# A decode block's last weight row: 640 columns by nine GpSimd transfers to twenty partitions

## The chip, the core and the metric

The kernel runs on one core of a Trainium2 chip. The metric is the time of one execution on the device in microseconds (us). The profile's span runs from the first to the last instruction of one profiled execution.

## What is computed

One decode step of a transformer block: layernorm, grouped attention over a long cache, output projection and residual, then layernorm, a gated feed-forward part and residual. Cut to what matters here:

```python
def _B_ref(x, w_gate, w_up, w_down):
    return (_gelu(x @ w_gate) * (x @ w_up)) @ w_down

h  = x + _A_ref(_layernorm(x), k_cache, v_cache, wq, wo)   # one token, 32 heads over 65536 keys of 4 kv heads
h2 = h + _B_ref(_layernorm(h), w_gate, w_up, w_down)       # D = 1024, F = 3584, all bf16
```

Nearly all of the work is to read the cache and the weights once: 173 MB. `w_down` has 3584 rows of 1024 columns.

## The kernel before

SyncE issues nearly all loads, in the order of use: `wq`, then key and value chunks of 4 to 8 MB, `wo`, `w_gate`, `w_up` and `w_down`. They go through a ring of four 32 KB slots in each partition. Each load is issued as soon as the reader of its slot is done, so several stand in the queue ahead of their use. The attention is a loop of eight steps on TensorE, VectorE and ScalarE. An explicit list of operations with semaphores (`Flow`) sets the order up to the gate matmuls; from line 583 on the order of each engine is the order in the text.

The end of the program is what the change touches:

- `w_down` is laid out as 28 rows for each of 128 partitions. `FA` = 16 of them form `wa`, the other `FB` = 12 `wb_src`, of which the first `FM` go to `wb` and the last `FZ` - 1 to `w_end`. The twelfth, `last_row`, is split by columns at `EC` = 640.
- Columns 640 to 1023 of `last_row` come first in SyncE's queue, by four transfers of three partitions with ten slots each and two of four partitions (line 600, semaphore 0). They lie in `w_odd`, on partitions 0 to 11 in eleven slots, in the memory of the transposed keys (`over` places a tensor there). Row 12 s + m of the 128 is slot s of partition m.
- Then come `wa` (semaphore 1, 4096 KB), `wb` (semaphore 2), two rows of `w_end` (semaphore 3), and columns 0 to 639 of `last_row` on 128 partitions (semaphore 4, 160 KB).
- When `up` has landed, 64 matmuls (L646) make its product, VectorE turns it into columns (L623) and multiplies it into `actz` (L649), the activations.
- For `w_odd` the activations of the last row have to be moved: `s_of` and `g_of`, made at the start from the identity, tell for each partition its slot and its place. VectorE masks (L682), one matmul gathers (L683), VectorE copies into `a_odd` (L684), and eleven matmuls (L689) use it.
- `down_wide` (L669): 32 matmuls, 512 wide, on `wa`, into the bank `e_ps`. ScalarE copies the bank into `e_sb` (L694), while `stay_busy` runs three matmuls whose result nobody reads (L662). `add_wide` (L675) folds `e_sb` into the output banks with four fp32 matmuls, which the trace shows as eight.
- `down` (L657): 128-wide matmuls into the output banks, eight for each row of 1024 columns, so 72 for nine rows, 16 for two and 5 for the last 640 columns. Each group waits for its own semaphore.
- Two copies (L704, L705) and a store (L706) end the program.
- GpSimd at that place clears `actz` (L618) and makes `to_row` and `h_of` (L615 to L617), on which the matmul of L637 waits. That matmul stands ahead of the 64 of L646 on TensorE.

Of the kernel before, what the change touches and what calls it, by code (L numbers as in the profile page):

```python
# [9 lines left out]
ALU = mybir.AluOpType  # L10
AX = mybir.AxisListType
BF16 = mybir.dt.bfloat16
# [106 lines left out]
def kernel(  # L119
# [13 lines left out]
    nc = tc.nc  # L133
    P = 128
# [7 lines left out]
    FC = F // P  # L142
# [13 lines left out]
    NB = 512  # L156
# [8 lines left out]

    FZ = 3
    w_end = nc.alloc_sbuf_tensor("w_end", [P, FZ, D], BF16)
# [14 lines left out]
    def sb(name, shape, dtype=F32):  # L182
        return const.tile(shape, dtype, name=name)
# [3 lines left out]
    qs = sb("qs", [P, 4, NS, P + 1], BF16)  # L187
    sc = sb("sc", [P, CPH, NN, rep, NS])
    pt = sb("pt", [P, CPH, NN, rep, NS], BF16)
    bank = [psum.tile([P, NB], F32, name="bank%d" % i) for i in range(8)]  # L190
    kt_bytes = ktb[:].rearrange("p c s w -> p (c s w)")

    def over(offset, shape, dtype=F32):

        n = 1
        for x in shape:
            n *= x
        if dtype == F32:
            v = kt_bytes[:, offset // 4:offset // 4 + n]
        else:  # L200
            v = kt_bytes[:, offset // 4:offset // 4 + n // 2].bitcast(BF16)
        if len(shape) == 2:
            v = v.rearrange("p (a b) -> p a b", a=shape[0])
        return v
# [5 lines left out]
    op = f.op  # L210
# [4 lines left out]
    k_sem = [tc.alloc_semaphore("k_landed_%d" % i) for i in range(DCH)]  # L215
    end_sem = [tc.alloc_semaphore("end_landed_%d" % i) for i in range(5)]

# [38 lines left out]
    GN = 3 * GP  # L256
    GS = P // GN
    left = GS * GN
    ident_w = sb("ident_f", [P, GN * (GS + 1)])
    ident_f = ident_w[:, 0:P]  # L260

    def select(key, out, op_, fill, base, pattern, mult, rows=None):
# [14 lines left out]
       in_=ident_f.rearrange("p (q m) -> p q m", q=4).unsqueeze(2).to_broadcast([P, 4, NI, SQ]))  # L277
# [8 lines left out]
    op("dve", "tensor_reduce", r=["ident_f"], w=["mine"], out=mine[:], in_=ident_f.rearrange("p (i c) -> p i c", i=NI), axis=AX.X, op=ALU.add)  # L286
    g_of = sb("g_of", [P, GN], BF16)
    s_of = sb("s_of", [P, GS + 1], BF16)
    op("dve", "tensor_reduce", r=["ident_f"], w=["g_of"], out=g_of[:], in_=ident_w[:].rearrange("p (s m) -> p m s", m=GN), axis=AX.X, op=ALU.max)
    op("dve", "tensor_reduce", r=["ident_f"], w=["s_of"], out=s_of[:], in_=ident_w[:].rearrange("p (s m) -> p s m", m=GN), axis=AX.X, op=ALU.max)  # L290
    sel16 = sb("sel16", [P, 16])
# [288 lines left out]
    with tc.tile_critical(no_gpsimd_drain=True):  # L580
# [15 lines left out]
    loads += [(wa, B_w_down[0:P * FA, :].rearrange("(p e) n -> p e n", p=P), 1), (wb[:, 0:FM, :], wb_src[:, 0:FM, :], 2),  # L596
              (w_end[:, 0:FZ - 1, :], wb_src[:, FM:FB - 1, :], 3), (w_end[:, FZ - 1, 0:EC], last_row[:, 0:EC], 4)]
    landed = [0] * 5
    for dst, src, i in loads:
# [17 lines left out]
    nc.gpsimd.tensor_tensor(out=h_of, in0=h_col[:].unsqueeze(1).to_broadcast([P, 16, DC]), in1=sel16[:].unsqueeze(2).to_broadcast([P, 16, DC]), op=ALU.mult)  # L617
    nc.gpsimd.memset(actz, 0.0)  # L618

    def columns(r):  # L620
# [38 lines left out]

    def stay_busy(n):  # L660
        for i in range(n):
            nc.tensor.matmul(bank[5][:], lhsT=qs[:, 0, 0, 0:P], rhs=qs[:, 1 + i % 3].rearrange("p s c -> p (s c)")[:, 0:NB], start=True, stop=True)  # L662

    e_sb = sb("e_sb", [P, NB])

    def down_wide(a_row, w_row, e):
        for h in range(DS):
            q = 2 * (e % 2) + h
            nc.tensor.matmul(e_ps[32 * q:32 * q + 32, :], lhsT=a_row[:, AZ:AZ + 32], rhs=w_row[:, h * NB:(h + 1) * NB],  # L669
                             start=False, stop=False, skip_group_check=True, tile_position=(0, 32 * q))  # L670
# [6 lines left out]

    odd_ps = bank[4][0:GN, 0:GS + 1]
    a_of = sb("a_of", [P, GS + 1], BF16)
    a_odd = over(19968, [GS + 1, 32], BF16)  # L680
    nc.gpsimd.memset(a_odd[0:GN], 0.0)
    nc.vector.tensor_tensor(out=a_of[:], in0=s_of[:], in1=actz[:, FC - 1, AZ:AZ + 1].to_broadcast([P, GS + 1]), op=ALU.mult)  # L682
    nc.tensor.matmul(odd_ps, lhsT=g_of[:], rhs=a_of[:], start=True, stop=True)  # L683
    nc.vector.tensor_copy(out=a_odd[0:GN, :, 0], in_=odd_ps)  # L684
    nc.tensor.wait_ge(end_sem[0], landed[0])
    for s in range(GS + 1):
        q = 2 * (s % 2) + 1
        n = min(GN, P - s * GN)
        nc.tensor.matmul(e_ps[32 * q:32 * q + 32, EC - NB:NB], lhsT=a_odd[0:n, s, :], rhs=w_odd[0:n, s, :], start=False, stop=False,  # L689
                         skip_group_check=True, tile_position=(0, 32 * q))  # L690
    nc.tensor.wait_ge(end_sem[1], landed[1])
    for e in range(FA):
        down_wide(actz[:, e, :], wa[:, e, :], e)
    nc.scalar.copy(out=e_sb[:], in_=e_ps[:])  # L694
    stay_busy(3)
    add_wide()
    e = FA
    for i, w_rows in ((2, wb[:, 0:FM, :]), (3, w_end[:, 0:FZ - 1, :]), (4, w_end[:, FZ - 1:FZ, 0:EC])):
        nc.tensor.wait_ge(end_sem[i], landed[i])
        for r in range(w_rows.shape[1]):  # L700
            down(actz[:, e, :], w_rows[:, r, :])
            e += 1
# [34 lines left out]
```

## Time and profile before

| | |
|---|---|
| median of 3 runs | 409.47 us (409.17 to 409.49) |
| the profiled execution | 409.19 us, span 407.5 us |
| TensorE busy | 225.0 us (55%), mean granted clock 0.799 |
| VectorE busy | 201.6 us (49%) |
| ScalarE, GpSimd busy | 40.3 us (10%), 14.6 us (4%) |
| read from HBM | 173.02 MB, 425 GB/s over the span |
| last load issued to landing seen | 380.51 to 402.93 us in the chain |
| store issued | 405.29 us |

How to read it: times in the timeline are in us from the start of the span. "PE" is TensorE's matmul, "PEld" its weight load, "DVE" VectorE, "ACT" ScalarE, "POOL" GpSimd, "SP" SyncE; a "q" behind the name is the engine's sequencer, which issues and waits. In a group of instructions the parts are: line, engine, operation, out<-in, shape, count, and behind the bar busy time, mean time of one, and idle time ahead with what ended it. A window gives its length, busy time and count for each of the five engine parts, the granted TensorE clock, the share of the sixteen DMA engines that was busy, and GB/s. A row of DMA issues ends in KB and in the us from issue to landing. Beside these views the trace keeps a record for every packet that a DMA engine moved: queue, start, duration, bytes.

### The profile page before, as it was taken

Reading aid. Unit: us, or ns where it says so; the run is one execution under the profiler, and the core shown is the slowest. Engines: PE = TensorE matmul, PEld = TensorE weight load, DVE = VectorE, ACT = ScalarE, POOL = GpSimd, SP = SyncE. Lnnn points to the kernel's source line nnn. Section 1 sums busy time; section 2 is a strip of 40 time slices with the busy share of each in tenths; the row PEclk is TensorE's granted clock in tenths of the full one; section 3 lists DMA queues with packets and bytes.
Section 4 is the critical chain, followed back from the end, with each engine's and each line's share of the span. In section 5 each row is a group of like instructions: output and inputs, shape, how many; then the busy total and the mean of one; then the engine's idle time right before and its main releaser. Section 6 shows DMA issues by size and latency. Waiting matters only on the chain. (4 is left out here: it accounts for less than half of the span.)

```text
span 407.5 us, 3807 instructions
## 1 busy us (share of the span) xinstructions
PE 225.0 (55%) x1549; PEld 98.7 (24%) x1549; DVE 201.6 (49%) x164; ACT 40.3 (10%) x143; POOL 14.6 (4%) x27
## 2 busy tenths in 40 slices
PE   0433745684566278725872586378456637625066
PEld 0211312231222133203321232133223213222023
DVE  4128850885099328834862676188508930110210
ACT  1000003000400210031003000300040022000000
POOL 4010000001000000010000001000000000000100
PEclk9965995699689866968896889589868986676578
DMA  8999999999999999999998999999999999999995
GB/s 357 415 447 426 441 434 412 460 418 429 437 460 418 412 437 483 412 415 415 483 437 373 454 421 447 421 457 418 412 447 473 412 415 415 467 450 407 412 419 223
DMA packets 5105, 173.10 MB, mean 425 GB/s; under 512 B 616, under 2 KB 876, under 8 KB 1004
## 3 DMA queue, kind: packets, MB, share of 16 engines
q1 hardware_dynamic: 5052, 173.02, 98.6%
q8 instruction: 4, 0.07, 0.1%
q10 hardware_dynamic: 48, 0.00, 0.0%
q14 instruction: 1, 0.01, 0.0%
HBM read 173.02 MB, written 0.00 MB: 425 GB/s over the span
## 5 line engine op out<-in xcount | busy, mean ns | idle before, releaser
L105 DVE STREAM_TRANSPOSE ktb<-ring 128x4096 f32<-128x4096 f32 x32 | 141.2, 4419 | 74.6 <-DMA ring<-in_A_k_cache_dram 74.6
L464 PE MATMUL bank<-ktb,qs 128*128 128x512 bf16 x512 | 129.9, 412 | 54.1 <-PEq L450 54.1
L464 PEld LDWEIGHTS bank<-ktb,qs 128*128 128x128 bf16 x512 | 50.9, 103 | 129.8 <-issue 82.8
L476 PE MATMUL bank<-ring,pt 128*32 128x512 bf16 x512 | 43.9, 519 | 38.0 <-PEq L450 38.0
L423 ACT ACTIVATE pt<-sc,nb 128x256 bf16<-128x256 f32 x64 | 31.5, 494 | 257.3 <-ACTq L419 257.3
L105 DVE STREAM_TRANSPOSE sc<-bank 128x512 f32<-128x512 f32 x32 | 22.3, 695 | 36.1 <-PE bank L464 36.1
L476 PEld LDWEIGHTS bank<-ring,pt 128*32 128x32 bf16 x512 | 18.7, 126 | 60.0 <-issue 56.0
L105 PE MATMUL bank<-ring,xz 128*32 128x512 bf16 (+1 forms) x128 | 12.0, 551 | 17.1 <-DMA ring<-in_B_w_gate_dram 9.9
L105 DVE TENSOR_REDUCE mx<-sc 128x8 f32<-128x2048 f32 x8 | 18.3, 2286 | 0.3
L468 PE MATMUL bank<-ident_f,mx 128*8 128x128 f32 x8 | 2.5, 308 | 25.8 <-PEq L450 25.8
L105 POOL COPY qs<-qsel 128x512 bf16<-128x512 bf16 x4 | 5.3, 1326 | 235.6 <-PE bank L464 220.0
L485 PE MATMUL bank<-sel,acc_sb 128*128 128x8 f32 x64 | 8.2, 255 | 6.9 <-PEq L450 6.9
L423 ACT ACTIVATION_READ_ACCUMULATOR pt<-sc,nb x64 | 12.0, 187 | 0.0
L485 PEld LDWEIGHTS bank<-sel,acc_sb 128*128 128x128 f32 x64 | 7.7, 191 | 10.6 <-issue 10.6
L105 PEld LDWEIGHTS bank<-ring,xz 128*32 128x32 bf16 x128 | 4.5, 133 | 23.4 <-issue 14.4
L646 PE MATMUL bank<-ring,xz 128*32 128x512 bf16 (+1 forms) x64 | 4.9, 484 | 8.7 <-PEq L641 8.7
L427 ACT COPY acc_sb<-bank 128x512 f32<-128x512 f32 x8 | 4.7, 585 | 47.4 <-ACTq L426 47.4
L623 DVE STREAM_TRANSPOSE ktb<-bank 128x512 f32<-128x512 f32 (+1 forms) x4 | 2.3, 620 | 13.1 <-PE bank L646 13.1
L468 PEld LDWEIGHTS bank<-ident_f,mx 128*8 128x8 f32 x8 | 0.7, 83 | 29.5 <-issue 29.5
L105 DVE STREAM_TRANSPOSE ktb<-bank 128x512 f32<-128x512 f32 x2 | 1.3, 696 | 12.6 <-PE bank L105 12.6
L628 DVE MEMSET bank<- 128x512 f32 x1 | 0.5, 485 | 14.2 <-SPq L580 14.2
L470 PE MATMUL bank<-diag,ones_f 8*128 8x8 f32 x16 | 3.7, 299 | 5.7 <-PEq L450 5.7
(112 smaller groups left out, 69.8 us busy)
## 6 DMA issues: line engine op xcount, KB each, us to landing
ring<-in_A_k_cache_dram SPq DMA_DIRECT2D x16, 4096.0 KB, 25.1
ring<-in_A_wq_dram SPq DMA_DIRECT2D x2, 4096.0 KB, 16.7
ring<-in_A_wo_dram SPq DMA_DIRECT2D x2, 4096.0 KB, 25.1
ring<-in_B_w_gate_dram SPq DMA_DIRECT2D x1, 7168.0 KB, 24.1
ring<-in_B_w_up_dram SPq DMA_DIRECT2D x1, 7168.0 KB, 31.6
ring<-in_B_w_down_dram SPq DMA_DIRECT2D x1, 4096.0 KB, 17.3
ring<-in_B_w_down_dram SPq DMA_DIRECT2D x1, 2304.0 KB, 22.4
w_end<-in_B_w_down_dram SPq DMA_DIRECT2D x1, 512.0 KB, 23.2
```

What stands on the lines that cost most here:

```text
L105: ins = getattr(self.eng[e], o["call"])(**o["kw"])
L423: m = nc.scalar.activation(out=pt[:].rearrange("p c n h s -> p (c n) h s")[:, :, r, :], in_=sc[:].rearrange("p c n h s -> p (c n) h s")[:, ...
L427: nc.scalar.copy(out=acc_sb[:], in_=acc[:]).then_inc(from_act, 1)
L464: m = nc.tensor.matmul(bank[c][:], lhsT=qs[:, jt].rearrange("p s c -> p (s c)")[:, s * P:(s + 1) * P], rhs=mv[:, :, J, :, u], start=(s == ...
L468: nc.tensor.transpose(out=mxT_ps, in_=mx1[:], identity=ident_f).then_inc(s_step, 1)
L470: nc.tensor.matmul(bc_ps, lhsT=ones_f[0:rep, :], rhs=diag[:], start=True, stop=True).then_inc(s_step, 1)
L476: m = nc.tensor.matmul(acc[32 * q:32 * q + 32, :], lhsT=pt[:, c, n, :, :].rearrange("p h s -> p (h s)"), rhs=v_sb[:, c, :, n, :], start=(c ...
L485: m = nc.tensor.matmul(o_ps, lhsT=acc_sb[:, u * Dh:(u + 1) * Dh], rhs=sel[:, u:SQ:NS], start=(u == 0), stop=(u == NS - 1))
L623: nc.vector.transpose(out=r[:, o:o + n].rearrange("p (e j) -> p e j", j=32), in_=ps.rearrange("p (j e) -> p e j", j=32))
L628: nc.vector.memset(e_ps[:], 0.0)
L646: nc.tensor.matmul(f_banks[t // 4][32 * q:32 * q + 32, :], lhsT=hz[:, ci, :], rhs=w, start=(ci == 0), stop=(ci == DC - 1), tile_position=( ...
```

## The change

Columns 0 to 639 of `last_row` no longer end SyncE's queue. They come in `w_far`, on partitions 64 to 83 in seven slots (`HN` = 20 partitions, `HS` = 6 full slots and one of eight rows), by transfers that GpSimd issues after it has cleared `actz`, `a_odd` and the new `a_far`: one of eight partitions, then four of five partitions with six slots, and behind each of these a `step` transfer of 32 bytes to each of 11, 11, 11 and 3 partitions, whose data nobody reads. All nine count on a new semaphore 5. In the built program GpSimd issues the first of the nine ahead of `to_row` and `h_of`, the other eight behind them; and VectorE makes `d_odd` (after the matmul of L637) ahead of the steps for `gl`, where it stood behind them.

Fourteen new matmuls, for each slot one of 512 and one of 128 columns, use these weights. They stand behind `down_wide` and ahead of ScalarE's copy of `e_ps`, and wait for semaphore 5. The helper matmul and VectorE operations for the activations are now a function, called for `near` (as before) and for `far`. The function stay_busy goes. `FZ` is 4: `wb` has eight rows, `w_end` two and then one whole row, so that the last group has eight matmuls.

```diff
-    FZ = 3
+    FZ = 4
...
+    HP = 4
+    HN = 5 * HP
+    HS = P // HN
+    H0 = 64
+    ident_w = sb("ident_f", [P, max(GN * (GS + 1), HN * (HS + 1))])
...
-    op("dve", "tensor_reduce", r=["ident_f"], w=["g_of"], out=g_of[:], in_=ident_w[:].rearrange("p (s m) -> p m s", m=GN), axis=AX.X, op=ALU.max)
-    op("dve", "tensor_reduce", r=["ident_f"], w=["s_of"], out=s_of[:], in_=ident_w[:].rearrange("p (s m) -> p s m", m=GN), axis=AX.X, op=ALU.max)
+    def places(name, n, slots):
+        col, row = sb(name + "_col", [P, n], BF16), sb(name + "_slot", [P, slots], BF16)
...
+    near, far = places("near", GN, GS + 1), places("far", HN, HS + 1)
...
-              (w_end[:, 0:FZ - 1, :], wb_src[:, FM:FB - 1, :], 3), (w_end[:, FZ - 1, 0:EC], last_row[:, 0:EC], 4)]
-    landed = [0] * 5
+              (w_end[:, 0:2, :], wb_src[:, FM:FM + 2, :], 3), (w_end[:, 2:FZ - 1, :], wb_src[:, FM + 2:FB - 1, :], 4)]
+    h_left = HS * HN
+    w_far = over(0, [HS + 1, EC], BF16)
+    far_src = last_row[0:h_left, 0:EC].rearrange("(s i j) n -> j i s n", s=HS, j=HP)
+    step = sb("step", [P, HP * 16], BF16)
+    far_loads = [(w_far[H0:H0 + P - h_left, HS, :], last_row[h_left:P, 0:EC])]
+    for j in range(HP):
+        n = 11 if j < HP - 1 else 3
+        far_loads += [(w_far[H0 + j:H0 + HN:HP, 0:HS, :], far_src[j]), (step[0:n, 16 * j:16 * j + 16], last_row[0:n, 0:16])]
+    landed = [0] * 6
...
+    a_odd = over(19968, [GS + 1, 32], BF16)
+    a_far = over(20736, [HS + 1, 32], BF16)
+    nc.gpsimd.memset(a_odd[0:GN], 0.0)
+    nc.gpsimd.memset(a_far[H0:H0 + HN], 0.0)
+    for dst, src in far_loads:
+        d = nc.gpsimd.dma_start(out=dst, in_=src)
+        d.then_inc(end_sem[5], 16)
+        landed[5] += 16
...
-    nc.vector.tensor_tensor(out=a_of[:], in0=s_of[:], in1=actz[:, FC - 1, AZ:AZ + 1].to_broadcast([P, GS + 1]), op=ALU.mult)
-    nc.tensor.matmul(odd_ps, lhsT=g_of[:], rhs=a_of[:], start=True, stop=True)
-    nc.vector.tensor_copy(out=a_odd[0:GN, :, 0], in_=odd_ps)
+    acts(near, bank[4][0:GN, 0:GS + 1], a_odd[0:GN, :, 0])
...
+    acts(far, bank[3][H0:H0 + HN, 0:HS + 1], a_far[H0:H0 + HN, :, 0])
     nc.tensor.wait_ge(end_sem[1], landed[1])
     for e in range(FA):
         down_wide(actz[:, e, :], wa[:, e, :], e)
+    nc.tensor.wait_ge(end_sem[5], landed[5])
+    for s in range(HS + 1):
+        n = min(HN, P - s * HN)
+        for h, (c0, c1) in enumerate(((0, NB), (NB, EC))):
+            q = 2 * (s % 2) + h
+            nc.tensor.matmul(e_ps[32 * q:32 * q + 32, 0:c1 - c0], lhsT=a_far[H0:H0 + n, s, :], rhs=w_far[H0:H0 + n, s, c0:c1], start=False, stop=False,
+                             skip_group_check=True, tile_position=(H0, 32 * q))
     nc.scalar.copy(out=e_sb[:], in_=e_ps[:])
-    stay_busy(3)
     add_wide()
     e = FA
-    for i, w_rows in ((2, wb[:, 0:FM, :]), (3, w_end[:, 0:FZ - 1, :]), (4, w_end[:, FZ - 1:FZ, 0:EC])):
+    for i, w_rows in ((2, wb[:, 0:FM, :]), (3, w_end[:, 0:2, :]), (4, w_end[:, 2:FZ - 1, :])):
```

## The prediction

> **What bounds the kernel now.** I read the page's DMA rows first, then the chain that ended last, then the timeline and short windows of the last 10 us, then the DMA issues, and at last the single packets in the trace's DMA records. The page says that one queue (q1, SyncE's) moves nearly everything and that the DMA engines are full from start to end:
>
> ```profile
> DMA  8999999999999999999998999999999999999995
> ...
> q1 hardware_dynamic: 5052, 173.02, 98.6%
> ```
>
> The chain ends in the last load, the final 21 small matmuls, a copy and the store:
>
> ```profile
> 380.51 22.42 DMA ring<-in_B_w_down_dram
> 402.93 0.04 issue
> 402.97 1.19 PE bank L657 x72
> 404.16 0.04 issue
> 404.20 0.73 PE bank L657 x21
> 404.94 0.02 issue
> 404.96 0.26 ACT h L705
> ```
>
> So the end is set by when the last `w_down` bytes land. But the last microseconds are not full (us, then busy times by engine, granted clock, DMA share, GB/s):
>
> ```profile
> 401.00:402.00 1.00, 1.00 (x7) 0.65 (x8) 0.00 (x0) 0.00 (x0) 0.00 (x0) 0.52 0.89 355
> 402.00:403.00 1.00, 0.32 (x10) 0.07 (x10) 0.00 (x0) 0.00 (x0) 0.00 (x0) 1.00 0.58 214
> 403.00:404.00 1.00, 1.00 (x72) 0.99 (x72) 0.00 (x0) 0.00 (x0) 0.00 (x0) 1.00 0.42 161
> ```
>
> A share of 0.58 and then 0.42 means that about half of the sixteen engines are done. The packet records show which: a load gives each engine an equal share, yet eight engines finish their last 1280-byte packet at 402.1 to 402.5 and eight at 403.7 to 404.12. Four of the late ones were held up by an instruction fetch (16 KB records at 33.1, 353.8 and 376.8 us, an 8 KB one at 92.6; a 16 KB one costs its engine about 1.55 us); a fifth is held by the fetch at 401.06. Three more carry the 768-byte packets of the row's last 384 columns (40 each at 33 ns, 1.3 us). The kernel waits for the late half.
>
> **The change, part by part.** The sum is made against the profiled execution: span 407.5, time 409.19, that is 1.69 outside the span; the median is 409.47, 0.28 above it.
>
> The 160 KB transfer leaves the end of SyncE's queue: eight packets of 1280 B on every engine, 52 ns apart in the records, so 8 x 0.052 = 0.42 us earlier on the late engines. The split of the other rows (8 + 2 + 1 rows where it was 9 + 2) moves the same bytes: nothing. Those 128 packets now come on GpSimd's queue, 8 in one transfer and 30 in each of four, of five partitions. If a five-partition transfer uses five engines (the three-partition ones of L600 use three, by the records), each carries 24 x 0.052 = 1.25 us more.
>
> Every engine also gets entries that carry next to nothing: nine completions, and the four `step` transfers of 32-byte pieces. Small records of this trace take 9 to 11 ns, so at most 14 x 10 ns = 0.14 us on the late engines. The last load feeds eight matmuls and not five, 1.19 / 72 = 0.0165 us each: +0.05. If the five engines are early ones, the end moves by -0.42 + 0.14 + 0.05 = **-0.23 us**. They then end at about 402.5 - 0.42 + 1.25 = 403.3, still ahead of 403.8.
>
> TensorE's own work must fit under that:
>
> ```profile
> 397.45 2.58 PE L669 MATMUL bank<-ring,ktb 128*32 128x512 bf16 x32 [0.92 <-DMA ring<-in_B_w_down_dram]
> ...
> 399.96 1.46 PE L662 MATMUL bank<-qs 128*128 128x512 bf16 x3
> ...
> 400.07 0.58 ACT L694 COPY e_sb<-bank 128x512 f32<-128x512 f32 x1 [20.95 <-PE bank L669]
> ...
> 401.36 0.93 PE L675 MATMUL bank<-e_sb,fold 128*64 128x128 f32 x8
> ```
>
> The three dummy matmuls (1.46 us) go; they ran while ScalarE copied `e_sb`, and held the fold matmuls from 400.7 to 401.36. Fourteen new ones, seven 512 wide and seven 128 wide, now stand ahead of that copy. The wide ones use two column groups, as do the eleven 384-wide ones of L689, which took 1.15 us at full clock. So 1.0 us at full clock; at the 0.5 granted in 400 to 401 (L669 starts 13 matmuls a microsecond there and 24 before) about 1.35. I take 1.35, for the clock stage is the same: 400.03 + 1.35, copy and its handover 0.65, fold 0.93, then 64 + 16 matmuls at 0.0165, 1.32: 404.3. The last eight start when their row is seen: it lands at 403.8, and the trace has 0.48 us from the last packet of a load (404.12) to its matmul (404.60): 404.3. TensorE and the load come out level, so no gain of over 0.2% (0.82 us, about what a measurement of this kernel can tell from no change) is left: even with the load no bound, all 88 matmuls after a 1.0 us far part end near 404.1, 0.8 earlier.
>
> Covered edits: GpSimd issues one transfer ahead of `to_row` and `h_of`, on which L637 waits, and all of the up matmuls are behind L637; TensorE idles 8.66 us there, from 379.6 to 388.21. VectorE now makes `d_odd` before the gate's `gl`, which isn't read until 394. No row shows a GpSimd transfer being issued. Bounds are 0.19 us (GpSimd's shortest row here) and 1.84 (SyncE's longest issue at L600); I take 0.8, SyncE's small transfers, so nine end near 387. The far activations add one matmul and two short VectorE operations (0.17, 0.17 and 0.19 by the near ones), inside the 0.92 us that TensorE waits ahead of L669. The two extra reductions run at 4 us, under the first load.
>
> **A wait that the change adds.** TensorE waits for all nine transfers after L669, at 400.0, and the copy, the fold and all 88 last matmuls stand behind that wait. When do they land? The nearest row is the only load on a second queue:
>
> ```profile
> x_in<-in_A_x_dram ACTq DMA_DIRECT2D x1, 2.0 KB, 7.6
> ```
>
> 2 KB took 7.6 us. In the records each engine gives it one 64-byte packet (5.98), then a whole 32768-byte packet of SyncE's (1.22 us), then the next (7.20). One packet a turn, then. The five engines get 24 pieces and nine completions, 33 entries. Ready from about 381, they find 2 turns before the up load ends, 9 in `wa` (to 395.9 with the added bytes), 9 in `wb` (to 400.8), the other 13 in the last rows: 402.9. If several pieces go in a turn (three 1280-byte ones, say: two turns for a transfer's pieces, 13 or 17 with the completions), they land between 397.4 and 400.1. Wait and end meet at a landing near 400.3 (404.89 less the steps summed under the first rival).
>
> The Trainium skill, DMA: Bandwidth & Descriptors, section on queues, rings and completion order, says that an engine drains a whole packet of typically 9 to 17 descriptors before it switches queues. The `x_in` records differ, with one data piece a turn, though from ScalarE and not from GpSimd. By the page's rule the nine are landed before the wait and the sum stays; by the row it is the first rival.
>
> **Rivals.** *Late landing.* One piece a turn: seen at 402.9 + 0.48, far matmuls 1.0, copy 0.65, fold 0.93, 88 matmuls 1.45: 407.4 against 404.89, where the last matmul ends now, so +2.5: 412.0 from the median. For it: `x_in`. Against it: that was another engine's queue. It decides from a landing after 400.3.
>
> *Wrong engines.* The five loaded engines include late ones, or the one fetched for at 401. A late engine then ends 1.25 - 0.42 + 0.14 = 0.97 later: with the last matmuls +1.0, 410.4. The fetched early one gives about +0.6. For it: no record ties an engine to a number, and five engines are late by fetches alone. Against it: eight of the sixteen have neither a fetch nor 768-byte packets, and five loads fit on them.
>
> The Trainium skill, same page, section on why a DMA increments its semaphore by 16, says that GpSimd's transfers take consecutive engines from a cursor that goes round, SyncE's the lowest ones. Sizes 8, then 5 and 11 three times, then 5 and 3 make 64, so by it each data transfer after the first falls on the same five engines, whichever the cursor's start makes them. The trace agrees for SyncE's three-partition loads, all on the same three engines; for GpSimd no run here shows it.
>
> *GpSimd itself.* Its first transfer takes over 8 us, or nine take over 2.5 us each: the up matmuls or the wait come late. +1 to +3. Nothing in the trace speaks for it.
>
> *More gain.* The load is levelled better and TensorE meets a full clock: -0.8, 408.6.
>
> **How the numbers follow.** No change, -0.23: 0.43, since half of the engines are free and one piece a turn is shown for another queue only; 409.47 - 0.23 = 409.2, own range 408.9 to 409.6. Late landing 0.25. Wrong engines 0.20, of which a quarter stays within 0.2%. GpSimd itself 0.05. More gain 0.07. Slower: 0.25 + 0.15 + 0.05 = 0.45; same: 0.43 + 0.05 = 0.48; faster 0.07. The range runs from 408.8, below which only the better levelled case lies, to 412.4, the late landing with the far matmuls at the half clock's 1.35.
>
> **What would show it.** Right: the wait ahead of the far matmuls is short, DMA shares in the last 2 us are higher and end 0.3 us earlier, the last chain still runs from the load into L657's successor. Late landing: TensorE idle for 3 us after the 32 wide matmuls, released by the `ktb` load. Wrong engines: `wa` seen later than 397.45, by about a microsecond, and the last load too. GpSimd: long issues, TensorE starting the up matmuls after 388.2. A change of more than 0.8 us downwards would mean that the floor of TensorE's work was wrong.

## The result: 4.6 us slower

The changed kernel takes 413.93 us (median of 4 runs, 413.85 to 414.25) where the kernel before takes 409.32 in the same comparison: ratio 1.0114, 95% interval 1.0097 to 1.0132. The prediction was 409.2, with a range up to 412.4. It is wrong in sign and size. The profiled execution took 413.93 us, span 412.0, so 1.93 lies outside the span, where it was 1.69 before; TensorE's mean granted clock is 0.785.

### The profile after

The DMA rows of the page, in the order queue, packets, MB, share:

```profile
DMA  8999989998999899989999999999999999999992
...
q1 hardware_dynamic: 5052, 172.86, 97.8%
q0 software_dynamic: 352, 0.17, 0.2%
```

SyncE's queue still fills the span. The new row is q0, GpSimd's: 352 packets, 22 for each of the sixteen engines, though only 128 pieces are moved. The packet records give the sizes: 20 packets of 5120 B (four pieces), 20 of 2560 B (two), 8 of 1280 B, 36 of 32 B, and 268 of 16 bytes or less: the completions, and packets on engines that have nothing to carry.

The chain that ended last, from its last step on GpSimd to the copy:

```profile
384.07 0.60 POOLq L766
384.66 19.61 DMA step<-in_B_w_down_dram
404.27 0.14 issue
404.41 1.04 PE bank L727 x7
405.48 0.59 ACT e_sb L729
406.07 0.04 issue
406.11 0.84 PE bank L701 x8
406.95 2.53 PE bank L687 x45
409.50 0.26 ACT h L739
```

Before, this chain ran from the last `w_down` load into the last 93 small matmuls. Now it runs through the last of GpSimd's transfers, which took 19.61 us from its issue, into the far matmuls (L727), ScalarE's copy, the fold (L701) and the last 88 matmuls (L687). SyncE's load is off the chain, although it ends later too: its last packet ends at 405.97, against 404.12.

The last microseconds in windows (us, busy times by engine, granted clock, DMA share, GB/s):

```profile
401.00:402.00 1.00, 1.00 (x14) 0.31 (x8) 0.00 (x0) 0.00 (x0) 0.00 (x0) 0.50 0.95 388
402.00:403.00 1.00, 1.00 (x12) 0.15 (x4) 0.00 (x0) 0.00 (x0) 0.00 (x0) 0.50 0.91 373
403.00:404.00 1.00, 0.14 (x4) 0.00 (x0) 0.00 (x0) 0.00 (x0) 0.00 (x0) 0.98 0.90 356
404.00:405.00 1.00, 0.59 (x13) 0.45 (x14) 0.00 (x0) 0.00 (x0) 0.00 (x0) 1.00 0.51 203
```

Two things moved. The half-empty end of the load (0.51) comes 2 us later than before. And TensorE, which ran the 72 small matmuls of `wb` in 403 to 404 before, is idle there now: it waits for semaphore 5. The groups say how long each part took (busy us, mean ns, idle ahead):

```profile
L695 PE MATMUL bank<-ring,ktb 128*32 128x512 bf16 x32 | 3.6, 628 | 1.3 <-DMA ring<-in_B_w_down_dram 1.3
L687 PE MATMUL bank<-ring,ktb 128*32 128x128 bf16 x64 | 1.9, 310 | 0.0
...
L701 PE MATMUL bank<-e_sb,fold 128*64 128x128 f32 x8 | 0.8, 342 | 0.7 <-ACT e_sb L729 0.7
L727 PE MATMUL bank<-ktb 20*32 20x512 bf16 x6 | 0.8, 375 | 1.3 <-DMA step<-in_B_w_down_dram 1.3
```

The timeline has the same parts in order (start, us, line, and the idle time ahead):

```profile
399.53 3.60 PE L695 MATMUL bank<-ring,ktb 128*32 128x512 bf16 x32 [1.30 <-DMA ring<-in_B_w_down_dram]
...
404.41 1.02 PE L727 MATMUL bank<-ktb 20*32 20x512 bf16 x14 [1.27 <-DMA step<-in_B_w_down_dram]
...
406.11 0.84 PE L701 MATMUL bank<-e_sb,fold 128*64 128x128 f32 x8 [0.68 <-ACT e_sb L729]
...
406.88 1.90 PE L687 MATMUL bank<-ring,ktb 128*32 128x128 bf16 x64
...
408.57 0.85 PE L687 MATMUL bank<-w_end,ktb 128*32 128x128 bf16 x24
```

From these the end of the last matmul, 409.46 against 404.89, splits as follows (us):

| step | before | after | difference |
|---|---|---|---|
| `wa` seen, wide matmuls start | 397.45 | 399.53 | +2.08 |
| the 32 wide matmuls | 2.58 | 3.60 | +1.02 |
| from their end to the fold's start | 1.33 | 2.98 | +1.65 |
| fold | 0.93 | 0.84 | -0.09 |
| from the fold's end to the last matmul's | 2.60 | 2.51 | -0.09 |

The 2.98 are 1.28 of waiting for the nine transfers, 1.02 of far matmuls and 0.68 of copy. The last row hides something: before, about 1.1 of the last 2.60 us were waits for the load (the 93 matmuls take 1.5 at the full clock, in e16); now they are 88 matmuls in a row, at half the clock.

Why is `wa` late? The DMA issues answer for GpSimd (KB each, median us from issue to landing):

```profile
ktb<-in_B_w_down_dram POOLq DMA_DIRECT2D x4, 37.5 KB, 14.8
step<-in_B_w_down_dram POOLq DMA_DIRECT2D x3, 0.3 KB, 14.7
...
step<-in_B_w_down_dram POOLq DMA_DIRECT2D x1, 0.1 KB, 19.6
```

The transfers were in flight from 381 to 403.7, all through `wa` and `wb`. In the packet records SyncE's packets are longer in this time. A 32768-byte packet of `wa` takes 1.216 us as a rule, and 1.3 to 1.67 while far pieces are moved; from 388 to 390.5, when the records hold a single packet of pieces, it is 1.21 to 1.32. **Lengthening** is from here on the sum, over all packets of `up`, `wa` and `wb`, of what each takes above its usual time (2.118, 1.216 and, for `wb`, 0.612 or 0.688 us). It is 1.5 us before and 26.7 after: 1.6 us more for each of the sixteen engines.

### The profile page after: what moved, and what is told of

Its sections match the earlier page's. It is cut to its first block, busy times and chain, and to the rows that moved or that the text cites. A ratio compares the mean times of both kernels' runs of the same rounds, so it can differ in the third digit from the quotient of the medians.

```text
span 412.0 us, 3839 instructions
## 1 busy us (share of the span) xinstructions
PE 229.3 (56%) x1556; PEld 100.8 (24%) x1556; DVE 201.8 (49%) x168; ACT 40.3 (10%) x143; POOL 20.2 (5%) x37
## 5 line engine op out<-in xcount | busy, mean ns | idle before, releaser
L105 PE MATMUL bank<-ring,xz 128*32 128x512 bf16 (+1 forms) x128 | 12.9, 584 | 16.5 <-DMA ring<-in_B_w_gate_dram 9.6
L676 PE MATMUL bank<-ring,xz 128*32 128x512 bf16 (+1 forms) x64 | 5.3, 511 | 7.5 <-PEq L671 7.5
L105 DVE STREAM_TRANSPOSE ktb<-bank 128x512 f32<-128x512 f32 x2 | 1.3, 696 | 12.5 <-PE bank L105 12.5
```

What stands on the lines that cost most here:

```text
L105: ins = getattr(self.eng[e], o["call"])(**o["kw"])
L676: nc.tensor.matmul(f_banks[t // 4][32 * q:32 * q + 32, :], lhsT=hz[:, ci, :], rhs=w, start=(ci == 0), stop=(ci == DC - 1), tile_position=( ...
```

## The experiments

Times are medians with the ratio's 95% interval in brackets; the kernel before measured 409.13 to 409.25 in these comparisons.

### Which part of the transfers delays the load

**e1_unread**: the kernel before, with all nine transfers, and nobody reads them.

```diff
+    for dst, src in far_loads:                  # w_far and step as in the change
+        d = nc.gpsimd.dma_start(out=dst, in_=src)
+        d.then_inc(end_sem[5], 16)
...
+    nc.tensor.wait_ge(end_sem[5], landed[5])    # at the very end
```

> The kernel before, with the same nine GpSimd transfers added at the same place of GpSimd's queue, into memory that nobody reads; SyncE still loads the 160 KB, TensorE's work is that of before. Turns theory (every GpSimd transfer takes turns on all sixteen DMA engines, with its pieces or with empty packets, and the SyncE packet behind each is stretched; 26 us of stretch and 10 us of own packets in the changed kernel's records, over 16 engines 1.7 + 0.6): wa is seen near 399.5 and not at 397.45, the load's end moves by about +2.3, the time to 411 to 412. Wrong-engines theory (only the five engines with data lose time, 1.25 each): +0 to +1.3, 409.3 to 410.6, and stretch only where there is data. TensorE theory (the new matmuls, the missing dummy matmuls and the clock cost the time): nearly nothing, 409.3 to 409.7.

411.78 us [1.0046, 1.0080], +2.5.

```profile
399.51 3.61 PE L692 MATMUL bank<-ring,ktb 128*32 128x512 bf16 x32 [1.10 <-DMA ring<-in_B_w_down_dram]
...
405.14 1.19 PE L680 MATMUL bank<-ring,ktb 128*32 128x128 bf16 x72 [0.23 <-DMA ring<-in_B_w_down_dram]
406.38 0.69 PE L680 MATMUL bank<-w_end,ktb 128*32 128x128 bf16 x21
```

`wa` is seen at 399.51, as in the change, and the lengthening is 25.7. So the transfers alone delay the load by 2 us, whoever reads them. This is about half of the loss: of the 2.5, some 0.4 is that the 160 KB are read twice here (e5).

**e2_sync_slots**: the change, with the far pieces as seven SyncE transfers ahead of the other `w_down` loads, no GpSimd transfer and no step.

```diff
+    loads = [(w_far[H0:H0 + min(HN, P - s * HN), s, :], last_row[s * HN:min(P, (s + 1) * HN), 0:EC], 5) for s in range(HS + 1)] + loads
-    for dst, src in far_loads:
-        d = nc.gpsimd.dma_start(out=dst, in_=src)
```

> The changed kernel, with the same w_far loaded by SyncE in seven transfers, one for each slot (20 partitions, ten engines by the rule that held for L600's, and one of 8), ahead of its other w_down loads; no GpSimd transfer and no step. TensorE's work stays that of the changed kernel. Turns theory: the loss goes; the load ends at 404.12 - 0.42 + up to 0.62 on ten engines, so 409.2 to 409.8. Wrong-engines theory: also near before, 409.2 to 410. TensorE theory: most of the loss stays, 412 to 414.

411.65 us [1.0041, 1.0090]; two of the five executions, the profiled one among them, took 413.8, the others 411.1 to 411.65. In the profile no packet goes on GpSimd's queue, yet the lengthening is 21.0, nearly all of it while the far and near pieces are in flight: four packets of `up` take 3.1 to 3.3 us in place of 2.12, and the first 23 of `wa` 1.5 to 2.6. So it isn't GpSimd's queue that lengthens packets.

**e3_one_transfer**: the kernel before, its 160 KB transfer issued by GpSimd instead of SyncE.

```diff
-              (w_end[:, 0:FZ - 1, :], wb_src[:, FM:FB - 1, :], 3), (w_end[:, FZ - 1, 0:EC], last_row[:, 0:EC], 4)]
+              (w_end[:, 0:FZ - 1, :], wb_src[:, FM:FB - 1, :], 3)]
...
+    d = nc.gpsimd.dma_start(out=w_end[:, FZ - 1, 0:EC], in_=last_row[:, 0:EC])
```

> The kernel before, with its last transfer (128 partitions, columns 0 to 639) issued by GpSimd where the changed kernel issues the first of its nine; the consumers are those of before. Turns theory, price by pieces: each engine gets 8 pieces in two packets and a completion, so 0.4 of its own and 2 x 0.37 stretch, less the 0.42 that leaves the end: +0.7, 410.0. Turns theory, price by transfers: one instead of nine, 3 turns and not 22: +0.2 or less, 409.1 to 409.5. Wrong-engines theory: equal shares, no change, 409.3. In all of them the bytes land before 390, ahead of their use.

409.50 us [0.9999, 1.0019]: no difference. The same bytes by the same queue, in 48 packets, to 128 partitions: lengthening 2.3. Here the 160 KB are moved by the same engines in equal shares, only earlier, and that gains nothing: the last packet ends at 404.36.

**e4_no_step**: the change without the four `step` transfers.

```diff
-        far_loads += [(w_far[H0 + j:H0 + HN:HP, 0:HS, :], far_src[j]), (step[0:n, 16 * j:16 * j + 16], last_row[0:n, 0:16])]
+        far_loads += [(w_far[H0 + j:H0 + HN:HP, 0:HS, :], far_src[j])]
```

> The changed kernel without the four step transfers: five GpSimd transfers. Turns theory: 14 turns and not 22, so the landing that TensorE waits for comes by 399 to 400 and the 1.28 us wait ahead of the far matmuls goes; if only packets with several pieces stretch SyncE's, wa stays at about 399.2 and the time is 412 to 412.8; if each turn costs alike, wa is seen at 398.8 and the time is near 411.5. Wrong-engines theory: the five-partition transfers now go round over other engines (0.31 us on each of up to fifteen engines and not 1.25 on five), so the load's end falls back to within 0.5 of before and the time to 409.5 to 410.

414.11 us [1.0104, 1.0138], with one execution of five, the profiled one, at 411.97. In that one the last piece lands at 400.4, and nothing waits ahead of the far matmuls; the lengthening is 27.5. So the late landing comes from the turns that the steps take, and the lengthening does not. Why the median did not follow is left to the clock, below: in the profiled execution it is 1.0 from 403.9 to the end, and the last 88 matmuls take 1.5 us; the others have no profile.

**e5_front_128**, **e6_front_64to83**, **e7_front_spread**: the kernel before, with 160 KB more from SyncE, unread, ahead of the `w_down` loads: by one transfer to 128 partitions, by seven to partitions 64 to 83, by seven to partitions 12, 18, ... 126.

```diff
+    w_far = over(21248, [EC], BF16)     # e5
+    loads = [(w_far, last_row[:, 0:EC], 5)] + loads     # e5
...
+    loads = [(w_far[64:64 + min(HN, P - s * HN), s, :], last_row[s * HN:min(P, (s + 1) * HN), 0:EC], 5) for s in range(HS + 1)] + loads     # e6
...
+    loads = [(w_far[12:13 + 6 * (min(HN, P - s * HN) - 1):6, s, :], last_row[s * HN:min(P, (s + 1) * HN), 0:EC], 5) for s in range(HS + 1)] + loads     # e7
```

> The kernel before, and ahead of its w_down loads SyncE also issues the 160 KB (columns 0 to 639 of last_row) once more, by one transfer to all 128 partitions, unread. It is the control of the next two runs: the bytes cost 8 x 0.052 = 0.42 us on every engine. All theories: about 409.6 us, wa seen 0.4 us later than before (397.9), the 32768-byte packets of wa lengthened by under 2 us in sum. If the place in the queue is what hurts, it is near 411.3.

> As e5, but the 160 KB go to partitions 64 to 83 in seven slots, by seven SyncE transfers of 20, 20, 20, 20, 20, 20 and 8 pieces, unread. Theory 'few partitions' (several engines that write to the same few partitions hold up all sixteen): wa seen near 399.5, 32768-byte packets lengthened by 12 to 18 us in sum, 411 to 411.7 us. Rival 'half clock' (e2's loss came from the far matmuls and the clock alone, the longer packets being made up later): within 0.3 us of e5.

> As e6, the same seven SyncE transfers of the same pieces from the same source rows, but to 20 partitions that lie six apart (12, 18, ... 126). Theory 'few partitions, side by side': no lengthening worth telling, within 0.3 us of e5 (409.6). Rival 'many small transfers' (what costs is that 128 pieces come by seven transfers with their own completions, uneven over the engines, and not where they land): as e6, 411 or more.

e5: 409.62 [1.000, 1.002], lengthening 1.9: the added bytes cost their 0.4 us, and the place in the queue nothing. e6: 411.49 [1.0037, 1.0070], lengthening 21.6. e7: 410.79 [1.0023, 1.0048], lengthening 9.7, in between and as neither theory had it. It is also disturbed: SyncE issued `wa` and `wb` at 386.1 to 387.0, against 380.9 to 381.7 in e5, so that the queue ran nearly dry at 386 (92 GB/s in 386 to 387; a mean DMA share of 0.40 over 384 to 387, against 0.85 before). e7 alone doesn't decide.

**e8_steps_only**: the kernel before, with nine unread GpSimd transfers of eleven 32-byte pieces.

```diff
+    far_loads = [(step[0:11, 16 * j:16 * j + 16], last_row[0:11, 0:16]) for j in range(9)]
```

> The kernel before, and nine GpSimd transfers of 11 pieces of 32 bytes each after the clearing of actz, unread; no far pieces. Theory 'turns' (each GpSimd transfer costs all sixteen engines two turns of their own, whatever it carries): 18 turns at 20 to 50 ns, 0.4 to 0.9 us later, 409.6 to 410.1, wa's packets lengthened by 5 to 10 us in sum. Theory 'few partitions': 32-byte pieces are too short to hold anybody up, 409.2 to 409.5, lengthened by under 3 us.

410.21 us [1.0013, 1.0033]; lengthening 2.4. The queue's row on its page:

```profile
q0 software_dynamic: 288, 0.00, 0.0%
```

Eighteen packets on each engine for 99 pieces of 32 bytes: two for every transfer, on all sixteen engines. The last packet of the load ends at 404.55, 0.43 later than before, or 24 ns a turn on the engine that ends last. That is the theory of turns, and its size: in the change 22 turns are worth about 0.5 us of the 2. The time itself is 1.0 longer than before. The last matmul ends 0.6 later, and 2.04 us lie outside the span (median), where the kernel before has 1.74.

**e10_unread_spread**: e1 with the pieces sent to partitions six apart, SyncE's queue being full this time.

```diff
-    far_loads = [(w_far[H0:H0 + P - h_left, HS, :], last_row[h_left:P, 0:EC])]
+    far_loads = [(w_far[12:13 + 6 * 7:6, HS, :], last_row[h_left:P, 0:EC])]
...
-        far_loads += [(w_far[H0 + j:H0 + HN:HP, 0:HS, :], far_src[j]), (step[0:n, 16 * j:16 * j + 16], last_row[0:n, 0:16])]
+        far_loads += [(w_far[12 + 6 * j:13 + 6 * j + 96:24, 0:HS, :], far_src[j]), (step[0:n, 16 * j:16 * j + 16], last_row[0:n, 0:16])]
```

> e1_unread once more (the kernel before, and the nine GpSimd transfers, unread; 411.78 us, 16.2 us of lengthening in wa's packets), with the pieces sent to partitions 12, 18, ... 126 in place of 64 to 83; SyncE's queue is full while they come, other than in e7. Theory 'few partitions, side by side': lengthening under 6 us in sum, 410.0 to 410.6 us, what is left being the turns. Rival 'uneven small pieces' (it is enough that some engines carry small pieces while others carry large ones): 14 to 18 us and 411.6 to 412.

411.48 us [1.0040, 1.0074], lengthening 20.7 against 25.7. Where the twenty partitions lie matters little: "few partitions, side by side" falls.

**e12_one_to_sixteen**, **e15_one_to_64**, **e16_row_order**: one unread GpSimd transfer beside the kernel before, to 16 partitions of eight slots, 64 of two, and to 128 partitions with the source rows in e12's order.

```diff
+    far_loads = [(over(0, [8, EC], BF16)[H0:H0 + 16], last_row[:, 0:EC].rearrange("(s i) n -> i s n", s=8))]     # e12
...
+    far_loads = [(over(0, [2, EC], BF16)[H0:H0 + 64], last_row[:, 0:EC].rearrange("(s i) n -> i s n", s=2))]     # e15
...
+    far_loads = [(over(21248, [EC], BF16)[:], last_row[:, 0:EC].rearrange("(s i) n -> i s n", s=8))]     # e16
```

> The kernel before, and the 160 KB once more, unread, by one GpSimd transfer to sixteen partitions (64 to 79, eight slots): as few partitions as in the change, but each engine gets the same eight pieces at the same time, and there are no steps. Theory 'few partitions': lengthening of wa's and up's packets over 8 us in sum, 410.3 to 411.3 us. Rival 'uneven small pieces': as the transfer to 128 partitions (e3, e5), under 3 us, 409.5 to 409.8 us.

> e12_one_to_sixteen (one GpSimd transfer, unread, beside the kernel before; 411.04 us, up's and wa's packets lengthened by 18 us) with 64 partitions of two slots in place of 16 of eight. Theory 'number of partitions': lengthening in between, 2 to 9 us, 409.8 to 410.4 us. Rival 'row order': the rows lie 64 apart within a partition; no forecast of its own, under 2 us of lengthening if only a stride of 16 rows hurts.

> The 160 KB once more by one unread GpSimd transfer to all 128 partitions, but the source rows in the order of e12 (0, 16, 32, ... 112, 1, 17, ...), so that an engine reads rows 16 apart. Theory 'number of partitions': nothing, as e5: 409.5 to 409.8 us, lengthening under 3 us. Rival 'row order': as e12, 410.5 to 411.3 us, over 10 us.

e12: 411.04 [1.0028, 1.0062], lengthening 18.5. e15: 410.76 [1.0021, 1.0050], 12.5. e16: 410.65 [1.0023, 1.0048], 15.7. All three have 32 packets of 5120 B and 16 completions on q0, as e3, so the turns are the same. e16 is the surprise: 128 partitions, one transfer, and it hurts like e12. It shares GpSimd's queue with e3 and the added bytes with e5; what neither of them has is the order of the source rows. So a small set of partitions isn't needed for the lengthening; for a single transfer the order in which the rows of `w_down`, 24 KB apart, are read is enough. It isn't the only way: in e2 and e6 each transfer reads twenty consecutive rows (the last one eight), and the lengthening is 21 to 22.

**e17_rows_in_order**: the change, with six consecutive rows on each far partition; the activations are gathered to match.

```diff
-    far_src = last_row[0:h_left, 0:EC].rearrange("(s i j) n -> j i s n", s=HS, j=HP)
+    far_src = last_row[0:h_left, 0:EC].rearrange("(i j s) n -> j i s n", s=HS, j=HP)
```

> The changed kernel, with the far rows laid out so that each of the 20 partitions reads six consecutive rows (row 6 m + s is slot s of partition m; the activations are gathered to match), in place of rows 20 apart. Same transfers, partitions, engines, steps. Theory 'row order': packets of up and wa lengthened by under 6 us in sum (27 in the changed kernel), wa seen near 398.1, the wait for the nine stays: 411.5 to 412.5 us with TensorE at the half clock. Rival 'small pieces on some engines': as the changed kernel, wa seen at 399.5, 413.5 to 414.3.

415.41 us [1.0144, 1.0178], lengthening 23.9 against 26.7, `wa` seen at 399.43: the order of rows, changed in this way, does not help the five-partition transfers. It is even slower than the change. Its profiled execution is the fastest of four, at 414.38; its span is the change's, 412.0, and its 0.45 us more lie outside the span. The other three have spans of 413.1 to 413.9, and no profile says why.

**e11_early**: the change, with the nine transfers issued by GpSimd at the start, into memory of their own.

```diff
     layernorm_cols("x_col", x_col[:], "xz", xz[:, :, 0], "ln1")
...
+    for dst, src in far_loads:
+        f.dma("pool", dst, src, r=["neg_half"], sem=end_sem[5])
```

> The changed kernel, with the nine transfers issued at the start, into memory of their own, so that they land in the first key loads. Theory 'paid wherever they lie': the loads behind them shift by the 1.8 us on every engine that the change costs now, wa seen again near 399.5, but no wait ahead of the far matmuls (1.3 us less): 412.0 to 412.7 us. Rival 'paid only at the end' (early on the stream makes it up, or small pieces do not hold up the key loads): wa seen near 397.5, 409.5 to 410.5 us.

411.71 us [1.0040, 1.0074], executions from 411.20 to 412.90. The pieces land by 43.6 us. At the end the lengthening is 1.7, but `wa` is seen at 399.56: the delay of 2 us is there already when TensorE begins the `up` matmuls (390.27 against 388.21). In 16 to 44 us the 32768-byte packets are 23 us longer in sum. The cost of the pieces is paid at the start as at the end: the load stream has no slack here to make it up. The profiled execution is the slowest of the four, 412.90, 1.0 below the change: what it saves is the wait.

### What TensorE loses

**e9_no_far_loads**: the change without the nine transfers and the wait for them; the far matmuls use what lies in the memory, and 160 KB are not loaded.

> The changed kernel without the nine transfers and without the wait for them: columns 0 to 639 of the last row are not loaded, and the fourteen far matmuls run on what lies in the memory. It shows TensorE's side of the change alone. Theory 'the loads lose it' (as the prediction's sum for TensorE): wa seen near 397.5, the last matmul at 404 to 405, 409 to 409.7 us. Rival 'TensorE's longer chain loses it': with the granted clock at 0.5 after wa the wide matmuls take 3.6, the far ones 1.9, the 88 last ones 2.5, the last matmul ends at 406.3 to 407.2, 410.8 to 411.8 us.

411.26 us [1.0037, 1.0071], +2.0 without any far load. TensorE's timeline (start, us, line, and the idle time ahead):

```profile
397.59 2.86 PE L685 MATMUL bank<-ring,ktb 128*32 128x512 bf16 x32 [0.90 <-DMA ring<-in_B_w_down_dram]
400.38 1.88 PE L716 MATMUL bank<-ktb 20*32 20x512 bf16 x14
402.95 1.12 PE L691 MATMUL bank<-e_sb,fold 128*64 128x128 f32 x8 [0.68 <-ACT e_sb L718]
404.00 1.90 PE L677 MATMUL bank<-ring,ktb 128*32 128x128 bf16 x64
405.69 0.85 PE L677 MATMUL bank<-w_end,ktb 128*32 128x128 bf16 x24
```

`wa` is in time and the load ends at 403.87, yet the last matmul ends at 406.54. The granted clock is 0.50 in every window from 398.5 to the end. At this clock the chain of far part (1.88), copy, fold and last matmuls is the bound.

**e13_busy_again**: e9 with the three dummy matmuls back behind the copy. **e14_no_busy**: the kernel before without them.

```diff
+    stay_busy(3)        # e13, on e9
-    stay_busy(3)        # e14, on the kernel before
```

> e9_no_far_loads (the changed kernel without the nine transfers, the far matmuls running on stale data; 411.26 us) with the three dummy matmuls back in their place, behind ScalarE's copy. Theory 'the dummies hold the clock': the granted clock is 1.0 again from about 402, the last 88 matmuls take 1.5 us in place of 2.53, 409.3 to 410.2 us. Rival 'the far matmuls are simply in the way': the clock stays at 0.5, the dummies hold the fold for another 0.5 to 0.8 us, 411.5 to 412.2.

> The kernel before without its three dummy matmuls, nothing else. Theory 'the dummies hold the clock': the granted clock stays at 0.5 after 402, the last 93 matmuls take 2.5 to 2.7 us, 410 to 410.7 us. Rival 'the far matmuls are in the way': the fold begins 0.1 to 0.7 us earlier, the end is set by the load as before, 409.0 to 409.4 us.

e14: 410.05 us [1.0006, 1.0025], +0.86 for taking out three matmuls whose result nobody reads. Its timeline shows the reason:

```profile
397.71 3.60 PE L669 MATMUL bank<-ring,ktb 128*32 128x512 bf16 x32
402.01 1.12 PE L675 MATMUL bank<-e_sb,fold 128*64 128x128 f32 x8 [0.69 <-ACT e_sb L694]
403.06 2.11 PE L657 MATMUL bank<-ring,ktb 128*32 128x128 bf16 x72
404.95 0.85 PE L657 MATMUL bank<-w_end,ktb 128*32 128x128 bf16 x21
```

The clock is 0.50 from 397 to the end, and the 93 small matmuls take 2.7 us, where at the full clock they take 1.5 (in e16). Two of its ten executions took 409.25 and 409.28, so the clock can come back without the dummies. e13 has it both ways: 411.65 us [1.0027, 1.0070], but ten executions in two groups, three at 408.92 to 408.94 and seven at 411.45 to 412.30. The profiled one is of the first group:

```profile
397.42 3.06 PE L689 MATMUL bank<-ring,ktb 128*32 128x512 bf16 x32 [0.99 <-DMA ring<-in_B_w_down_dram]
400.41 1.52 PE L720 MATMUL bank<-ktb 20*32 20x512 bf16 x14
401.86 0.82 PE L682 MATMUL bank<-qs 128*128 128x512 bf16 x3
402.62 0.66 PE L695 MATMUL bank<-e_sb,fold 128*64 128x128 f32 x8
403.20 1.08 PE L677 MATMUL bank<-ring,ktb 128*32 128x128 bf16 x64
404.11 0.51 PE L677 MATMUL bank<-w_end,ktb 128*32 128x128 bf16 x24
```

Here the clock is back at 1.0 from 401.5, and every row behind the wide matmuls is shorter than in e9. So the far matmuls are no loss by themselves: with the clock granted, this kernel, which reads 160 KB less, is 0.25 us faster than the one before. The dummies don't ensure the clock (three of ten executions here, none of four in e9). That they make it likelier is shown by e14: with them 21 of the 22 executions of the kernel before lie under 409.7 us, without them two of ten.

**e18_order_busy_no_steps**: e17 with the dummies and without the steps.

> e17 without the four step transfers and with the three dummy matmuls back behind ScalarE's copy. If row order, turns and granted clock are all there is: wa seen near 398, no wait ahead of the far matmuls, last load byte near 404.2, and as in e13 two levels by the clock: 409 to 409.7 us where it is 1.0 from 402 on, 411.5 to 412.5 where it stays at 0.5. Rival 'something unnamed is left': none of its executions under 410.5 us.

411.69 us [1.0047, 1.0103], five executions: 411.18, 411.66, 411.69, 414.31, 414.47. 3.7 us of e17's time are gone, but no execution is under 410.5. The profile is of the slowest, 414.47, with the clock at 0.5 from 399.0 to 409.3; in it the lengthening is 28.6 and `wa` is seen at 399.99, so what is left is the lengthening and, in this execution, the clock. The cause that e17 and e18 were to remove is still in them. By its median, no version beat the kernel before.

## Why the prediction was wrong

**"Small records of this trace take 9 to 11 ns, so at most 14 x 10 ns = 0.14 us"**: this term was mis-sized. Every GpSimd transfer puts packets on all sixteen engines, data or not: 22 on each, and e8 measured 24 ns for each turn, 0.5 us in all.

**"Each carries 24 x 0.052 = 1.25 us more", on five engines**: the failed step, and the largest. The pieces were costed at their own time on the engines that carry them. What they cost is the time of everybody else's packets: 25 us of lengthening over what there was before, on all sixteen engines. The sum had the end 0.23 earlier; the load's last packet came 1.85 later, and `wa` 2.08. Of the latter, 0.46 is what 160 KB ahead of `wa` cost in any form (e5: last packet of `wa` at 397.41, against 396.95). *Wrong engines* named the sign that came true (`wa` and the last load late), but not the cause: by the records nine engines now end at about 403.8 to 404.5 and seven at 405.4 to 406.0, where it was eight at 402.5 or before and eight at 403.7 to 404.1. The levelling gained one engine, and the mean end went from about 403.1 to 404.8.

**"13 or 17 turns with the completions, landed between 397.4 and 400.1"**: 22 turns, landed at 403.7. The pieces do go several to a turn (four and two), not one as in the `x_in` row. The packets of the first transfer and of the four steps were missing from the count. So the wait that the first rival described did come, 1.28 us, by another way than it argued; that its landing of 402.9 lies near the measured one is luck. The Trainium skill, DMA: Bandwidth & Descriptors, section on queues, rings and completion order, calls 9 to 17 descriptors in a packet typical; the records of GpSimd's queue here show four or two pieces.

**"The clock stage is the same"**: no. The sum took a half for the far part and 1.0 from 402 on, as the profile before shows it. After the change the wide matmuls take 3.60 in place of 2.58, and the last 88 take 2.53, where 0.0165 each would make 1.45. The far part's price at the half clock was too low as well: 1.35 was taken, where the sum's own rows (13 starts in a microsecond, those of 399 to 400, against 24) make 1.85 of the 1.0, and e9 measured 1.88. That e13's fast executions lie 0.25 below the kernel before, and the forecast 0.23, is in part chance: e13 has the dummies and reads 160 KB less. That TensorE's part and the load come out level meant that it had no cover against the clock, and the text priced the half clock for the far matmuls alone, not for the fold and the last 88.

**The dummies, taken out at no cost**: they were read as matmuls that hold the fold until 401.36. e14 puts a price of 0.86 us on their removal.

**What was right**: GpSimd's issues (0.52 to 0.72 us each, 0.8 was taken) end at 385; the matmul that waits for GpSimd's work starts 1.6 us later than before and hides in TensorE's idle time; the two far operations and the split of the rows cost nothing. The 0.42 for 160 KB at the end of the load was right in size: where they aren't loaded at all, the last packet comes 0.25 (e9) and 0.40 (e13) earlier. In the change the pieces cost it again.

**How the losses add up**: the load alone costs 2.5 (e1), TensorE's side alone 2.0 (e9). That this makes 4.5 of the 4.6 measured is in part chance: e1 reads 160 KB twice (0.4), e9 doesn't read them once, and neither has the wait of 1.28. Of e1's 2.5, about 0.5 is turns (e8), 0.4 the added bytes (e5) and 0.3 time outside the span (2.01 against 1.74); the rest goes with the lengthening, 24 us over sixteen engines.

**What stays open**: why small reads hold up all engines. It isn't the queue (e2, e6), nor the place in it (e5), nor the completions (e8), and it needs no small set of partitions (e16). In one transfer to 128 partitions it follows the order of the rows; in the five-partition transfers one changed order didn't remove it. Nor do all small strided reads do it: the kernel before reads 128 pieces of 768 bytes, rows twelve apart on a partition, by three-partition transfers, beside packets of `up` and `wa` that keep their usual time. The Trainium skill, DMA: Bandwidth & Descriptors, section on latency and other measured facts, tells of copies whose rate falls by up to about half with the pitch of their rows in HBM, at pitches of 2 to 8 MiB, and infers that channels are hit in step. That the reading of rows can matter agrees with e16 against e5, at 24 KB; no run here shows a channel.

Open also is what grants the clock; that the dummies raise the odds is shown, how they do it is not. The Trainium skill, TensorE: Matmul & The Clock Gate, section on the clock gate, says that the clock is throttled by default and that some 3.4 us of activity release it. The dummies' effect has that sign. But in e8 TensorE was busy without a gap from 396.5 to 405.5, and the granted clock was 0.5 from 397.1 to 403.9. The clock records of every trace show one thing more: the granted clock changes on a grid of 3.41 us (before at 391.72, 398.55 and 401.96; after at 392.80, 396.21, 403.04 and 406.45), and the grid lies elsewhere in each execution. So the same matmuls can meet either clock; the wide ones of the kernel before had 1.1 us of the full clock, those of the change next to none. How far this explains the two levels of e13 is not shown.

## What to carry to other kernels

Where the load stream is the bound, the price of a small transfer can be far above its own bytes on its own engines: put it, unread, beside the kernel before, and look at how long everybody else's packets take. Before matmuls that "do nothing" are taken out of a stage with a changing granted clock, take them out alone. And a forecast in which two chains come out level needs a price for the case that the one on TensorE runs at the half clock.

## What the runs showed of the hardware that was not expected

- A GpSimd transfer of a few pieces makes packets on all sixteen engines: 18 for each by nine transfers that carry 99 pieces (e8), about 24 ns a turn on the engine that ends last.
- The same 160 KB in pieces of 1280 bytes cost their bytes alone when the rows are read in order by one transfer (409.62, e5), and 1.4 us more than before when one transfer reads them sixteen apart (410.65, e16).
- A packet of 32 KB can take 1.5 to 2.6 us in place of 1.22, also on engines whose records, in order, hold no small piece (e2).
- GpSimd transfers cost time outside the span too: 1.90 to 2.39 us (medians) in the runs with five or nine of them, 1.70 to 1.84 in those with one or none.
- Three matmuls without use are worth 0.86 us at the end of this kernel, through the granted clock (e14).
